# Decays as running products on VectorE, and the quarters of a product in other PSUM banks, in a scan layer followed by an ELU feed-forward layer

## The chip, the cores and the metric

The kernel runs on one core of one Trainium2 chip. The metric is device time in microseconds (us) of one execution. All matrices are fp32. The engines are named as in the profile: PE is TensorE (PEld its weight loads), DVE is VectorE, ACT is ScalarE, POOL is GpSimd, SP is the engine whose queue issues nearly all transfers.

## The reference, cut to what matters

```python
# x (4, 8, 768, 32), a (4, 8, 768) in 0.85..0.95, B and C (4, 8, 768, 16)
for c in range(24):                              # chunks of 32 tokens
    cum = np.cumsum(log(a)[chunk], axis=-1)
    L = np.exp(cum[..., :, None] - cum[..., None, :]) * causal
    y_intra = ((C @ B.T) * L) @ x
    y_inter = (C @ state) * np.exp(cum)[..., None]
    y[chunk] = y_intra + y_inter
    state = exp(sum(log a)) * state + sum_j(B_j x_j * exp(cum_last - cum_j))
h = y.transpose(0, 2, 1, 3).reshape(3072, 256) @ w_in      # w_in (256, 2048)
g = np.where(h > 0, h, np.exp(np.minimum(h, 0)) - 1)
out = g @ w_out                                            # w_out (2048, 256)
```

The entry L[i, j] of a chunk is the product of the decays a of the tokens j+1 to i, 1 where i is j, and 0 where i is before j. The chunk is free to choose as long as the state is carried right; the kernel uses chunks of 64.

## The kernel before, in words

**Blocks.** The 3072 tokens are cut into twelve blocks of 256, numbered n = 0 to 11. Each block is four chunks of 64 tokens (u and v, each 0 or 1) for eight heads. A block goes through two halves: the scan, which ends in `inside` (L542) with the turned output yT, and the feed-forward part, 8 steps i of 256 hidden columns each.

**The decays of a block.** For blocks 0 and 1 they are made from sums on PE and stay as they are. For blocks 2 to 11, `running_sums` (L273) takes cumulative sums F of log a once for all rows, `write_flat` (L308) puts them and their exponentials into DRAM, and `spread_cum` (L331) reads them back so that each of the 128 partitions (a token j) of the tile L holds the sums of all tokens i. `decay_of` (L436) then makes exp(cum_i - cum_j) by ACT, one instruction for each head and u with the sum of token j as the bias: 16 of 128x64 for a block (L439). POOL clears what lies before the diagonal with four `affine_select` of 64x512 for a block (L444). `ncum` and `eb`, the turned biases and the turned decays to the chunk's end, are made once (L906, L907). `scaled` (L359) multiplies B by the decay to the end, `weigh` (L463) multiplies the scores by L.

**The feed-forward part of blocks 0 to 3** is plain: `l1` (L577) makes a step's h, four matrix products of 128x256, and `l2` (L700) multiplies by w_out. In the trace each fp32 product is two matmul instructions.

**The feed-forward part of blocks 4 to 11** takes two blocks at a time (n = 4, 6, 8, 10) and does seven products in place of eight by Strassen's method in Winograd's form, for the first product in `front`, `front_sums`, `mid` and `back` (L660 to L692), for the second in `second` (L736). One step i of a pair of blocks is called a group here: there are 32 of them. A group has two PSUM banks, c1 and c2, of two quarters of 128x256 each. `front` issues three products and lets ACT copy the first of them. `front_sums` makes two sums by DVE in SBUF. `mid` issues two products and one DVE sum, `back` two products and two DVE sums. Only then are c1 and c2 both finished, and only then both enter the list `lag`, from which `elu` (L598) takes them: ACT makes relu(-h) (L596) and exp of it (L603), DVE makes g from this and h (L605).

**Order.** Everything is in the order in which the code is written (`manual_schedule`); each engine works through its own list in that order, and waits by semaphores. The loop at L1051 goes over the pairs, with 16 half steps k (k even: `front`, k odd: `mid` and `back`); between them it puts seven steps of `second` for the pair before (`l2s`), and what `scan_ahead` (L967) has for the next two blocks m and m+1: decays and the turning of B and C (`turn`, `turn_exp`) at k below 8, scores at k = 9, `weigh`, `sums` and `states` at k = 10 and 11, `across` and `inside` at k = 13. The pool of PSUM banks `p_a` has seven banks, taken in turn, so a new tile waits until the one seven takings before is free.

**Weights.** w_in and w_out come as fp64 words in 16 pieces, and are made fp32 by `w_take` (abs on ACT, the low word by L164 on ACT or L166 on DVE, the sign on DVE) and `w_give` (two DVE instructions L183 and L190, one sum L200 on POOL).

Of the kernel before, what the change touches and what calls it, by code (L numbers as in the profile page):

```python
# [10 lines left out]
F32 = mybir.dt.float32  # L11
# [17 lines left out]
def kernel(  # L29
# [234 lines left out]
    make_heads(1)  # L264

    def clip(t):
        nc.vector.tensor_scalar(
            out=t, in0=t, scalar1=1e-6, scalar2=1.0, op0=ALU.max, op1=ALU.min)
# [28 lines left out]
    F = const.tile([ROWS, 2, 2, P], F32, name="F")  # L297
    E = la

    def rest_of_sums():  # L300
        to_last(F[:, 0], E, nc.gpsimd)
        nc.scalar.activation(E, E, ACT.Exp)

# [26 lines left out]

    def spread_cum(n):  # L331

        st.setdefault(n, {})["L"] = L = att.tile([P, NH, 2, Q], F32, tag="L", name="L", bufs=2)
        for v in range(2):
            nc.sync.dma_start(
                out=L[Q * v:Q * v + Q].rearrange("p h u i -> p h (u i)"),
                in_=flat[v, rows_of(n)].rearrange("h u i -> h (u i)").unsqueeze(
                    0).to_broadcast([Q, NH, P]))

    def spread_exp(n):  # L340

        st.setdefault(n, {})["ec"] = ec = att.tile([P, 2, P], F32, tag="ec", name="ec", bufs=4)
        for h in range(NH):
            row = rows_of(n).start + NG * h
            nc.sync.dma_start(
                out=ec[N * h:N * (h + 1)].rearrange("n u i -> n (u i)"),
                in_=flat_exp[row:row + 1].to_broadcast([N, BLK]))

# [10 lines left out]
    def scaled(n, eng):  # L359

        s = st[n]
        s["sc"] = sc = att.tile([P, 2, NH, N], F32, tag="sc", name="sc", bufs=3)
        factor = eb0[:, :, NH * n:NH * (n + 1)] if n < 2 else eb[:, :, rows_of(n)]
        eng.tensor_tensor(
            out=sc, in0=s["bc"][:, 0],
            in1=factor.unsqueeze(3).to_broadcast([P, 2, NH, N]), op=ALU.mult)
# [64 lines left out]
    def decay(n, q):  # L431

        decay_of(n, 2 * q)
        decay_of(n, 2 * q + 1)

    def decay_of(n, h):  # L436
        L, row = st[n]["L"], rows_of(n).start + NG * h
        for u in range(2):
            nc.scalar.activation(  # L439
                L[:, h, u], L[:, h, u], ACT.Exp, bias=ncum[:, u, row:row + 1])  # L440
        if h % 4 == 3:
            for v in range(2):
                part = L[Q * v:Q * v + Q, h - 3:h + 1]
                nc.gpsimd.affine_select(  # L444
                    out=part, in_=part, pattern=[[0, 4], [0, 2], [1, Q]],
                    compare_op=ALU.is_ge, fill=0.0, base=0, channel_multiplier=-1)

# [212 lines left out]
    def front(n, i):  # L660
        c1, c2 = psum([P, 2, BLK], "ps_h"), psum([P, 2, BLK], "ps_h")
        t = y_sums[n]
        part_product(c1[:, 0], a11[:, i], yT[n // 2][:, 0, 0].rearrange("p u i -> p (u i)"), True)
        copy = conv.tile([P, BLK], F32, tag="sgn", name="p_copy")
        nc.scalar.copy(out=copy, in_=c1[:, 0])
        part_product(c2[:, 1], s_in[0][:, i], t[:, 1], True)
        part_product(c2[:, 0], a21[:, i], t[:, 0])
        open_[n, i] = c1, c2, copy

    def front_sums(n, i):  # L670
        c1, c2, copy = open_[n, i]
        u = conv.tile([P, 2, BLK], F32, tag="mag", name="u_sum")
        nc.vector.tensor_tensor(out=u[:, 0], in0=c2[:, 1], in1=copy, op=ALU.add)
        nc.vector.tensor_tensor(out=u[:, 1], in0=c2[:, 0], in1=u[:, 0], op=ALU.add)
        open_[n, i] = c1, c2, u

    def mid(n, i):
        c1, c2, u = open_[n, i]
        b21 = yT[n // 2][:, 1, 0].rearrange("p u i -> p (u i)")
        part_product(c1[:, 0], a12[:, i], b21)  # L680
        part_product(c1[:, 1], s_in[1][:, i], y_sums[n][:, 2])
        nc.vector.tensor_tensor(out=c2[:, 1], in0=c1[:, 1], in1=u[:, 1], op=ALU.add)  # L682

    def back(n, i):
        c1, c2, u = open_.pop((n, i))
        b22 = yT[n // 2][:, 1, 1].rearrange("p u i -> p (u i)")
        part_product(c1[:, 1], a22[:, i], y_sums[n][:, 3])
        part_product(c2[:, 0], s_in[2][:, i], b22)
        nc.vector.tensor_tensor(out=c1[:, 1], in0=c1[:, 1], in1=u[:, 0], op=ALU.add)  # L689
        nc.vector.tensor_tensor(out=c2[:, 0], in0=c2[:, 0], in1=u[:, 0], op=ALU.add)  # L690
        lag.append((n, i, c1))
        lag.append((n + 1, i, c2))  # L692
# [29 lines left out]
    def sub(out, in0, in1):  # L722
        nc.gpsimd.tensor_tensor(out=out, in0=in0, in1=in1, op=ALU.subtract)  # L723

    def sum_t1(n, i, eng=nc.gpsimd):
        b12 = g_of[n + 1, i][:, 0]
        eng.tensor_tensor(out=b12, in0=b12, in1=g_of[n, i][:, 0], op=ALU.subtract)  # L727

    def sum_t2(n, half):
        for i in range(4 * half, 4 * half + 4):  # L730
            t2_of[n, i] = ffn.tile([P, BLK], F32, tag="t2", name="t2", bufs=4)
            sub(t2_of[n, i], g_of[n + 1, i][:, 1], g_of[n + 1, i][:, 0])

    c_of = {}

    def second(n):  # L736
# [6 lines left out]
        for half in range(2):  # L743
# [8 lines left out]
            for r, a in enumerate((a11, a12, s1, s2, s3, a22, s4)):  # L752
                pool, tag = (p_a, "a") if (7 * half + r) % 2 else (p_o, "o")
                ps = pool.tile([P, 2, P], F32, tag=tag, name="ps_o")
                for i in chunk:
                    A, B = g_of[n, i], g_of[n + 1, i]
                    b = (A[:, 0], A[:, 1], B[:, 0], t2_of[n, i], A[:, 0], A[:, 1], B[:, 1])[r]
                    for ts in range(2):
# [6 lines left out]
                if r == 0:  # L765
                    nc.scalar.copy(out=p1, in_=ps)
                    for i in chunk:
                        sub(g_of[n, i][:, 0], t2_of[n, i], g_of[n, i][:, 0])
                    if half:
                        add(c11, c11, p1)  # L770
                elif r == 1:
                    add(c11, ps, c11 if half else p1)
                    for i in chunk:
                        sub(g_of[n, i][:, 1], g_of[n, i][:, 1], t2_of[n, i])
                elif r == 2:
# [61 lines left out]
    w_low(0, nc.scalar)  # L837
    log_of(la)
    scores(0)
# [21 lines left out]
    w_sum(1)  # L861
    running_sums(la, F[:, 0], ROWS)
    l1(0, 0)
# [4 lines left out]
    elu()  # L868
    nc.scalar.activation(F[:, 1], F[:, 0], ACT.Exp)
    write_flat()  # L870
    spread_cum(2)
    w_load(5)
# [15 lines left out]
    scaled(1, nc.gpsimd)  # L888
    rest_of_sums()
    w_give(3)  # L890
    make_heads(2)
    turn_exp(1)
    l1(0, 2)
# [11 lines left out]
    w_take(4, nc.vector)  # L905
    ncum = turned(F[:, 0], "ncum", -1.0, nc.vector)  # L906
    eb = turned(E, "eb", 1.0, nc.vector)  # L907
    w_give(4)
# [5 lines left out]
    for s, (n, i) in enumerate((  # L914
            (1, 0), (1, 1), (1, 2), (0, 4), (1, 3), (0, 5), (1, 4), (0, 6), (1, 5), (0, 7),
            (1, 6), (1, 7))):
        l1(n, i)
        if s < 8:
            decay_of(2, s)
        if s == 7:  # L920
# [3 lines left out]
        if s % 2 == 1 and todo < 10:  # L924
            w_take(todo, nc.vector)
            w_give(todo)
            w_load(todo + 6)
            todo += 1
        if s == 4:
            scaled(2, nc.gpsimd)  # L930
# [4 lines left out]
        if s == 8:  # L935
            spread_cum(3)
            load_x(3)
            spread_exp(3)
            weigh(2, 2)
            weigh(2, 3)  # L940

            st[0] = kept
            sums(2, 0, pool=p_o, tag="o", parts=(None, last))
            states(0, last)
            st.pop(0)
            states(2)
        if s == 10:
            spread_cum(4)
            inside(across(2), 2)
# [17 lines left out]
    def scan_ahead(n, i):  # L967
# [3 lines left out]
        if 4 < m < NP and n % 2 == 1 and i in (4, 5):  # L971
            spread_cum(m + i - 4)
        m = n + 2 - n % 2
        if 4 <= m < NP and n % 2 == 0:
# [3 lines left out]
            if i == 2:  # L978
                if m == 4:
                    spread_cum(5)  # L980
                load_x(m)
                load_x(m + 1)
            for k in (i,) if m == 4 else (i, i + 1) if i % 2 == 0 else ():
                if k >= 2:
                    decay(m + k // 6, (k - 2) % 4)
            if i in (5, 7):
                turn(m + i // 7)
                turn_exp(m + i // 7)
        if 4 <= m < NP and n % 2 == 1:
            if i == 0:  # L990
                scaled(m, nc.gpsimd)
                scaled(m + 1, nc.gpsimd)
            for k in (i,) if m == 4 else (i, i + 1) if i % 2 == 0 else ():
                if k < 2:
                    decay(m + 1, k + 2)
            if i == 2 and m == 4:
# [14 lines left out]
    for n in (2, 3):  # L1011
        for i in range(8):
            l2(n - 2, i)
            if todo < len(pieces):
                w_take(todo, nc.vector)
            end_of_two(n, 2 * i)
# [34 lines left out]
    for n in range(4, NP, 2):  # L1051
# [14 lines left out]
        for k in range(16):  # L1066
# [18 lines left out]
            elif m and i == 5:  # L1085
                l2s(2)
                mid(n, i)
                states(m)
                l2s(2)
                back(n, i)  # L1090
                states(m + 1)
                next_elu()
                begin_elu()
            else:
                mid(n, i)
                if i == 0 and n > 4:
                    store(n - 4, 0)
                    store(n - 4, 1)
                l2s(2)
                back(n, i)  # L1100

                if n == 4 and i < 4:
# [5 lines left out]
                l2s(1)  # L1108
                next_elu()
                begin_elu()  # L1110
            if m:
# [52 lines left out]
```

## Time and profile before

| | |
|---|---|
| median of 3 runs | 364.41 us (364.33 to 365.36) |
| span in the profile | 362.9 us |
| PE busy | 354.3 us, 98% |
| DVE, ACT, POOL busy | 242.2, 200.7, 227.1 us (67%, 55%, 63%) |
| decays by ACT, L439 | 160 instructions, 41.0 us |
| clearing by POOL, L444 | 40 instructions, 27.3 us |
| the low words by DVE, L166 | 12 instructions, 7.1 us |
| five sums of a group by DVE, L673, L674, L682, L689, L690 | 32 each, 13.5, 13.6, 13.8, 13.7 and 13.8 us |

Busy time of an engine is the union of its instructions. Matmuls overlap one another in the trace, so that PE is shown busy also where the next product has not been started as early as it could be; the distance from one start to the next tells more than the busy share.

### The profile page before, as it was taken

The numbers are of one execution on the slowest core, as the hardware profiler recorded it, in microseconds if no ns is written. First come the engines' busy times: TensorE is split into PE (matmuls) and PEld (weight loads), VectorE is DVE, ScalarE is ACT, GpSimd is POOL, SyncE is SP. The second block draws the span as 40 slices with busy tenths as digits, with TensorE's granted clock in tenths as the row PEclk, the third lists the DMA queues.
The fourth block names the chain that finished last, engine by engine and source line by source line (L and its number), as shares of the span: only waits on it lengthen the run. The fifth ranks groups of instructions, "written<-read, shape, count | busy, mean of one in ns | idle before, by whom it ended". The sixth has DMA issues, their size and how long they took to land.

```text
span 362.9 us, 10146 instructions
## 1 busy us (share of the span) xinstructions
PE 354.3 (98%) x3978; PEld 316.9 (87%) x3978; DVE 242.2 (67%) x547; ACT 200.7 (55%) x499; POOL 227.1 (63%) x366
## 2 busy tenths in 40 slices
PE   8899999999999999999999999999999999999996
PEld 5578778888888998898999998999989999999995
DVE  4989887972697668784567684666685666666212
ACT  4858969767435567635485735386735352534100
POOL 4454443663567896679457578567587555456893
PEclk9999999999999999999999999999999999999999
DMA  8877995563050560053530045540000100000001
GB/s 155 203 203 147 240 308 141 66 116 63 3 116 19 65 85 12 4 115 48 96 65 2 3 95 68 93 72 0 3 2 4 58 2 0 3 0 32 29 2 58
DMA packets 96239, 25.33 MB, mean 70 GB/s; under 512 B 77312, under 2 KB 92096, under 8 KB 96192
## 3 DMA queue, kind: packets, MB, share of 16 engines
q1 hardware_dynamic: 94016, 24.49, 33.0%
q8 instruction: 31, 0.51, 0.6%
q10 hardware_dynamic: 2176, 0.20, 0.4%
q14 instruction: 16, 0.13, 0.1%
HBM read 21.33 MB, written 3.34 MB: 68 GB/s over the span
## 4 chain that ended last, share of the span: by engine, by line
PE 81%; DVE 7%; ACT 3%; DMA 3%; SPq 2%; issue 2%; POOL 1%; ACTq 0%; DVEq 0%
PE ps_o L759 32%; PE ps_h L655 25%; PE ps_h L583 10%; PE ps_o L707 8%; SPq L112 2%; PE ps_g L459 1%; DMA w<-in_moe_w_in_dram 1%; DVE g L605 1%; PE ps_y L553 1%; ACT e L596 1%; PE ps_st L489 1%; ACT e L603 1%; DMA flat<-F 1%; DVE mag L183 1%; PE ps_y L534 1%
## 5 line engine op out<-in xcount | busy, mean ns | idle before, releaser
L596 ACT ACTIVATE e<-ps_h 128x512 f32<-128x512 f32 x96 | 56.5, 588 | 93.1 <-DVE ps_h L689 71.2
L605 DVE SCALAR_TENSOR_TENSOR g<-e,ps_h 128x512 f32<-128x512 f32 x96 | 65.3, 681 | 39.2 <-ACT e L603 35.8
L759 PEld LDWEIGHTS ps_o<-w_out,g 128*128 128x128 f32 x640 | 80.3, 192 | 3.3 <-issue 0.5
L759 PE MATMUL ps_o<-w_out,g 128*128 128x128 f32 x640 | 81.4, 275 | 0.0
L727 POOL TENSOR_TENSOR g<-g 128x256 f32<-128x256 f32 x34 | 24.8, 729 | 67.1 <-DVE g L605 67.1
L583 PE MATMUL ps_h<-yT,w_in 128*128 128x256 f32 x256 | 60.6, 383 | 2.5 <-POOL w_in L200 1.8
L603 ACT ACTIVATE e<-e 128x512 f32<-128x512 f32 x96 | 60.9, 634 | 2.2
L583 PEld LDWEIGHTS ps_h<-yT,w_in 128*128 128x128 f32 x256 | 47.8, 190 | 10.6 <-POOL w_in L200 2.8
L759 PE MATMUL ps_o<-w_sum,g 128*128 128x128 f32 x320 | 43.0, 275 | 0.0
L759 PEld LDWEIGHTS ps_o<-w_sum,g 128*128 128x128 f32 x320 | 41.1, 192 | 1.4
L439 ACT ACTIVATE L<-L,ncum 128x64 f32<-128x64 f32 x160 | 41.0, 338 | 0.0
L655 PE MATMUL ps_h<-y_sum,w_in 128*128 128x256 f32 x128 | 38.6, 383 | 0.7 <-DVE ps_h L682 0.7
L655 PE MATMUL ps_h<-y_sum,w_sum 128*128 128x256 f32 x128 | 38.5, 382 | 0.5 <-DVE g L605 0.5
L655 PE MATMUL ps_h<-yT,w_in 128*128 128x256 f32 x128 | 38.8, 385 | 0.0
L444 POOL TENSOR_SCALAR_AFFINE_SELECT L<-L 64x512 f32<-64x512 f32 x40 | 27.3, 682 | 13.1 <-ACT L L439 11.8
L707 PE MATMUL ps_o<-w_out,g 128*128 128x256 f32 x128 | 30.8, 383 | 0.0
L655 PEld LDWEIGHTS ps_h<-y_sum,w_sum 128*128 128x128 f32 x128 | 23.9, 190 | 5.3 <-DVE g L605 1.3
L723 POOL TENSOR_TENSOR g<-t,g 128x256 f32<-128x256 f32 x40 | 27.9, 729 | 0.8 <-PE ps_o L759 0.8
L723 POOL TENSOR_TENSOR t<-g 128x256 f32<-128x256 f32 x40 | 28.1, 736 | 0.2
L723 POOL TENSOR_TENSOR g<-g,t 128x256 f32<-128x256 f32 x40 | 27.9, 730 | 0.2
L707 PEld LDWEIGHTS ps_o<-w_out,g 128*128 128x128 f32 x128 | 23.7, 190 | 3.4 <-POOL L L444 0.2
L689 DVE TENSOR_TENSOR ps_h<-ps_h,u_sum 128x256 f32<-128x256 f32 x32 | 13.7, 429 | 18.3 <-PE ps_h L655 18.3
(109 smaller groups left out, 538.3 us busy)
## 6 DMA issues: line engine op xcount, KB each, us to landing
L<-flat SPq DMA_DIRECT2D x20, 256.0 KB, 5.3
w<-in_moe_w_in_dram SPq DMA_DIRECT2D x8, 512.0 KB, 5.2
w<-in_moe_w_out_dram SPq DMA_DIRECT2D x8, 512.0 KB, 6.1
xr<-in_x_dram SPq DMA_DIRECT2D x24, 128.0 KB, 3.4
out_dram<-c_sum SPq DMA_DIRECT2D x10, 256.0 KB, 2.1
bc<-in_B_dram SPq DMA_DIRECT2D x24, 64.0 KB, 4.4
bc<-in_C_dram SPq DMA_DIRECT2D x22, 64.0 KB, 3.4
ec<-flat_exp SPq DMA_DIRECT2D x72, 16.0 KB, 1.7
```

Source lines behind the costliest of these rows:

```text
L439: nc.scalar.activation(L[:, h, u], L[:, h, u], ACT.Exp, bias=ncum[:, u, row:row + 1])
L444: nc.gpsimd.affine_select(out=part, in_=part, pattern=[[0, 4], [0, 2], [1, Q]], compare_op=ALU.is_ge, fill=0.0, base=0, channel_multiplier=-1)
L583: nc.tensor.matmul(out=ps[:, j], lhsT=w_in[:, k, m * P:(m + 1) * P], rhs=yT[n // 2][:, k, n % 2].rearrange("p u i -> p (u i)"), start=(k = ...
L596: nc.scalar.activation(begun[0], lag[0][2], ACT.Relu, scale=-1.0)
L603: nc.scalar.activation(e, e, ACT.Exp, scale=-1.0)
L605: nc.vector.scalar_tensor_tensor(out=g_of[n, i], in0=e, scalar=1.0, in1=ps, op0=ALU.subtract, op1=ALU.max)
L655: nc.tensor.matmul(out=out, lhsT=lhsT, rhs=rhs, start=first, stop=True, skip_group_check=True)
L689: nc.vector.tensor_tensor(out=c1[:, 1], in0=c1[:, 1], in1=u[:, 0], op=ALU.add)
L707: nc.tensor.matmul(out=o_of[n][:, ts], lhsT=g_of[n, j][:, m % 2, ts * P:(ts + 1) * P], rhs=w_out[:, m], start=(m == 0 and ts == 0), stop=( ...
L723: nc.gpsimd.tensor_tensor(out=out, in0=in0, in1=in1, op=ALU.subtract)
L727: eng.tensor_tensor(out=b12, in0=b12, in1=g_of[n, i][:, 0], op=ALU.subtract)
L759: nc.tensor.matmul(out=ps[:, ts], lhsT=b[:, ts * P:(ts + 1) * P], rhs=a[:, i], start=(i == chunk[0] and ts == 0), stop=(i == chunk[-1]), s ...
```

## The change: what it does and what it is for

1. **Decays as running products.** `running_products` takes F[:, 1], the products of the a within a chunk, by one scan of a itself (no logarithm, no exponential), and F[:, 0], which is a with the first token of each chunk set to 0. The latter is spread over the partitions (`spread_a`). `decay` is then one DVE scan over two heads in place (state = state times a, plus `same`, which is 1 on the diagonal): it gives 0 before the diagonal, 1 on it and the products after it. Four of 128x256 for a block take the place of sixteen ACT and four POOL instructions. `ncum`, `eb` and four transposes are gone; `scaled` reads the last column of L. For two blocks at a time the scans are one in each half step k = 0 to 7.
2. **Low words on ACT.** The low words of pieces 5 to 15 (L164) move from DVE to ACT.
3. **Quarters in other banks, and joined sums.** c1 now is finished by the sum of `mid`, c2 by that of `back`. `front_sums` and the sum of `back` are one DVE instruction of 128x512 each instead of two of 128x256, so a group has three sums instead of five. c1 enters `lag` after `mid`, and its `elu` stands ahead of `back`.
4. **One transfer instead of eight** in `spread_exp`, and `sc` has two buffers instead of three.

```diff
-    def rest_of_sums():
-        to_last(F[:, 0], E, nc.gpsimd)
-        nc.scalar.activation(E, E, ACT.Exp)
+    nc.gpsimd.tensor_scalar(
+        out=F[:, 0], in0=keep[0:ROWS], scalar1=-1.0, scalar2=1.0, op0=ALU.mult, op1=ALU.add)
+    def running_products():
+        nc.vector.tensor_tensor_scan(
+            out=F[:, 1].rearrange("p c s -> p (c s)"),
+            data0=F[:, 0].rearrange("p c s -> p (c s)"),
+            data1=la.rearrange("p c s -> p (c s)"), initial=0.0, op0=ALU.max, op1=ALU.mult)
+        nc.gpsimd.tensor_tensor(out=F[:, 0], in0=la, in1=keep[0:ROWS], op=ALU.mult)
...
-        for h in range(NH):
-            row = rows_of(n).start + NG * h
-            nc.sync.dma_start(
-                out=ec[N * h:N * (h + 1)].rearrange("n u i -> n (u i)"),
-                in_=flat_exp[row:row + 1].to_broadcast([N, BLK]))
+        nc.sync.dma_start(
+            out=ec.rearrange("p u i -> p (u i)"),
+            in_=flat_exp[rows_of(n)].unsqueeze(1).to_broadcast([NH, N, BLK]))
...
-        factor = eb0[:, :, NH * n:NH * (n + 1)] if n < 2 else eb[:, :, rows_of(n)]
+        factor = (eb0[:, :, NH * n:NH * (n + 1)] if n < 2 else
+                  s["L"][:, :, :, Q - 1].rearrange("p h u -> p u h"))
...
-        decay_of(n, 2 * q)
-        decay_of(n, 2 * q + 1)
-    def decay_of(n, h):
...
+        part = st[n]["L"][:, 2 * q:2 * q + 2].rearrange("p k u i -> p (k u i)")
+        nc.vector.tensor_tensor_scan(
+            out=part, data0=part, data1=same.rearrange("p k i -> p (k i)"),
+            initial=0.0, op0=ALU.mult, op1=ALU.add)
...
-        copy = conv.tile([P, BLK], F32, tag="sgn", name="p_copy")
-        nc.scalar.copy(out=copy, in_=c1[:, 0])
-        part_product(c2[:, 1], s_in[0][:, i], t[:, 1], True)
-        part_product(c2[:, 0], a21[:, i], t[:, 0])
+        u = conv.tile([P, 3, BLK], F32, tag="mag", name="u_sum")
+        nc.scalar.copy(out=u[:, 0], in_=c1[:, 0])
+        part_product(c2[:, 0], s_in[0][:, i], t[:, 1], True)
+        part_product(c2[:, 1], a21[:, i], t[:, 0])
...
-        nc.vector.tensor_tensor(out=u[:, 0], in0=c2[:, 1], in1=copy, op=ALU.add)
-        nc.vector.tensor_tensor(out=u[:, 1], in0=c2[:, 0], in1=u[:, 0], op=ALU.add)
+        nc.vector.tensor_tensor(
+            out=u[:, 1:3], in0=c2, in1=u[:, 0].unsqueeze(1).to_broadcast([P, 2, BLK]), op=ALU.add)
...
     def mid(n, i):
-        part_product(c1[:, 1], s_in[1][:, i], y_sums[n][:, 2])
-        nc.vector.tensor_tensor(out=c2[:, 1], in0=c1[:, 1], in1=u[:, 1], op=ALU.add)
+        part_product(c2[:, 0], s_in[1][:, i], y_sums[n][:, 2])
+        nc.vector.tensor_tensor(out=c1[:, 1], in0=c2[:, 0], in1=u[:, 2], op=ALU.add)
+        lag.append((n, i, c1))
...
     def back(n, i):
-        part_product(c1[:, 1], a22[:, i], y_sums[n][:, 3])
-        part_product(c2[:, 0], s_in[2][:, i], b22)
-        nc.vector.tensor_tensor(out=c1[:, 1], in0=c1[:, 1], in1=u[:, 0], op=ALU.add)
-        nc.vector.tensor_tensor(out=c2[:, 0], in0=c2[:, 0], in1=u[:, 0], op=ALU.add)
-        lag.append((n, i, c1))
+        part_product(c2[:, 0], a22[:, i], y_sums[n][:, 3])
+        part_product(c2[:, 1], s_in[2][:, i], b22)
+        nc.vector.tensor_tensor(out=c2, in0=c2, in1=u[:, 0:2], op=ALU.add)
         lag.append((n + 1, i, c2))
...
-            w_take(todo, nc.vector)
+            w_take(todo, nc.scalar)
...
-            for k in (i,) if m == 4 else (i, i + 1) if i % 2 == 0 else ():
-                if k >= 2:
-                    decay(m + k // 6, (k - 2) % 4)
+            if m > 4:
+                decay(m + i // 4, i % 4)
+            elif i >= 2:
+                decay(m + i // 6, (i - 2) % 4)
...
                 mid(n, i)
+                begin_elu()
                 l2s(2)
+                next_elu()
                 back(n, i)
+                begin_elu()
...
                 l2s(1)
-                next_elu()
-                begin_elu()
```

## The prediction

> **What bounds the kernel now.** I read the chain first, then the starts of PE in a quiet stretch, then the waits of PE, then the busy time by stage. The page and its chain:
>
> ```profile
> PE 354.3 (98%) x3978; PEld 316.9 (87%) x3978; DVE 242.2 (67%) x547; ACT 200.7 (55%) x499; POOL 227.1 (63%) x366
> ...
> PE 81%; DVE 7%; ACT 3%; DMA 3%; SPq 2%; issue 2%; POOL 1%; ACTq 0%; DVEq 0%
> ```
>
> The end is set by PE. Whether it could be denser is read from the starts of one group (the timeline of PE):
>
> ```profile
> 123.55 0.60 PE L655 MATMUL ps_h<-yT,w_in 128*128 128x256 f32 x2
> 123.98 0.59 PE L655 MATMUL ps_h<-y_sum,w_sum 128*128 128x256 f32 x2
> 124.42 0.59 PE L655 MATMUL ps_h<-y_sum,w_in 128*128 128x256 f32 x2
> 124.85 1.95 PE L759 MATMUL ps_o<-w_out,g 128*128 128x128 f32 x16
> ...
> 129.70 0.60 PE L655 MATMUL ps_h<-yT,w_in 128*128 128x256 f32 x2
> ```
>
> A product of 256 columns starts every 0.434 us (two instructions of 0.216), a step of L759 every 0.445 (four of 0.111). A group is 7 x 0.434 + 7 x 0.445 = 6.15 us, and the trace has 129.70 - 123.55 = 6.15. So here PE has no slack, and no relief of another engine can bring anything. The change leaves PE's list as it is except for four small transposes. What it can bring lies only in starts that come late. Those with a wait behind them:
>
> ```profile
> PE ps_h L583 <- POOL w_in L200: 1.8, 2, 1.4
> PE ps_idle L215 <- DVE idle L210: 1.1, 1, 1.1
> PE ps_h L655 <- DVE ps_h L682: 0.7, 1, 0.7
> PE ps_h L655 <- DVE g L605: 0.5, 2, 0.3
> PE ps_h L583 <- DVE g L605: 0.4, 1, 0.4
> ```
>
> These idle times are short by the modelled end of the matmul before, so I took each start minus the usual distance from the start before. Beyond the first 12 us this gives nine late starts: 0.6 at 22.7 us, 0.65 at 43.2, 0.3 at 52.0, 0.25 and 0.83 at 139 to 142, 0.2 near 154, 0.36 at 167.6, 0.43 at 223.2, 0.21 at 265.1. Their sum is 3.8 us, 1% of the time, and that is the prize. The tail after the last matmul (3.5 us) is a sum and a store, and stays.
>
> How full the others are where the scans go (busy time in stretches; columns PE, PEld, DVE, ACT, POOL):
>
> ```profile
> 28.00:117.40 89.40, 88.84 (x1002) 75.48 (x1001) 69.53 (x147) 62.48 (x157) 47.66 (x75) 1.00 0.55 120
> 117.40:142.20 24.80, 24.13 (x166) 22.43 (x164) 17.10 (x38) 15.72 (x45) 21.93 (x35) 1.00 0.47 65
> ...
> 173.00:198.00 25.00, 25.00 (x173) 23.57 (x172) 16.44 (x36) 16.73 (x47) 14.68 (x22) 1.00 0.35 59
> ```
>
> **What the Trainium skill says.** "Perfetto Trace Analysis", Identifying the Most-Contended Engine: matmul busy share is no measure of the distance to the limit. The trace agrees: 98% busy and still 3.8 us late. "DVE: opcode table, instruction layouts, handler registers and perf-mode slots", Datapath and trigger behaviour: a scan runs at half throughput. The one scan of 128x256 here took 691 ns against 421 for a sum of that size. "SBUF — State Buffer", Who interferes with whom: a DVE instruction with two SBUF inputs and a POOL instruction that reads SBUF exclude each other for their whole length. The trace agrees: a sum L631 of 128x128 took 0.28 us with POOL quiet at 137.38 and 0.71 at 137.69 while POOL worked. The new scans have two SBUF inputs.
>
> **The change part by part.** Following instructions on DVE start about 0.08 us before the one ahead ends, so I use 0.60 for a row of 0.68, 0.33 for 0.42 and 0.61 for a scan of 0.69.
>
> ACT: minus 160 x 0.24 (the distance of L439 to L439) = 38 us, plus 11 low words at 0.77 (L164) = 8.5. POOL: minus 27.3, plus two sums at about 0.7. DVE: 40 scans x 0.69 = 27.6, minus 11 low words of 0.58 = 6.4, minus 32 x (0.42 + 0.42 - 0.68) x 2 = 10.2: plus 11 us. The new forms are not in the trace; a joined sum is bounded by 0.68 (L605, also 512 wide from PSUM) and 0.85 (two apart), I take 0.68.
>
> Start, to 28 us. The logarithm and exponential (0.42 each) leave ACT at places where it waits for PE; nothing. L282 (0.61 on POOL at 20.23) overlaps L183 on DVE, which takes 0.81 instead of about 0.45; without it the piece that PE waits for at 22.7 comes 0.3 sooner. Minus 0.3. The four transposes fill a stretch at 27.0 in which the next product waits for the copy of yT on ACT, which ends at 27.50; nothing.
>
> 28 to 117 us. A scan (0.61) takes the place of a low word (0.38 apart) on DVE; ACT gives up four L439 (0.96) and gets 0.68 for each. The wait at 43.2 is for a g after the fourth scan: plus 0.1. Around 52 only the low words go: minus 0.3. For blocks 3 to 5, eight scans of 4.9 us meet six low words of about 3 us less, but ACT's abs no longer stands behind eight L439, and POOL loses the L444; pieces come no later. Nothing. Fewer transfers in the queue of SP (8 x 0.46 us become one) bring L for block 5 sooner; nothing on PE.
>
> Groups from 117 us. The PE wait for `mid`'s sum is old: the product at 134.54 follows the sum that ended at 134.28, so DVE has 0.2 us of slack there. New is that the second product of `mid` waits for `front_sums`. Most of all, g of c1 now stands on DVE behind `mid`'s sum and waits 1.33 us for ACT (0.59 + 0.63 and gaps), with `back`'s sum, scans, `front_sums` and g of c2 queued behind it, and behind these the next `mid` sum. The cycle of waits of a group with scans: mid sum 0.47, relu and exp 1.30, g 0.60, back sum 0.72, relu of c2 0.49 and copy 0.42 on ACT (the scan of the odd half step, 0.61, lies beside them), front_sums 0.60, g 0.60, one sum of `second` 0.33, scan 0.61: 6.14, as much as PE needs. For pairs 6 and 8 (four groups each): nothing to 0.2 us lost each pair; I take 0.1. For pair 4 come the weight sums L631 (about 0.7 a group) and, in the last two groups, `ctm` and `cts` (0.93). Working through the DVE list of its first four groups with these numbers I get late starts of 0.1, 0.2, 0.4 and 0.6: 1.3 against the 1.1 that stands there now. Groups without scans need 5.5 us.
>
> The waits at 167.6, 223.2 and 265.1 are for a bank that g of the earlier c1 holds:
>
> ```profile
> 167.42 0.69 DVE L605 SCALAR_TENSOR_TENSOR g<-e,ps_h 128x512 f32<-128x512 f32 x1 [1.00 <-ACT e L603]
> 167.77 1.13 ACT L570 COPY yT<-ps_y 128x256 f32<-128x256 f32 x3
> 168.16 0.30 PEld L655 LDWEIGHTS ps_h<-y_sum,w_sum 128*128 128x128 f32 x2 [0.60 <-DVE g L605]
> ```
>
> With c1 finished by `mid`, this g is over some 2 us sooner. Minus 1.0.
>
> Sum: -0.3 + 0.1 - 0.3 + 0.2 (pair 4) + 0.2 (pairs 6 and 8) - 1.0 = -1.1, and a little from 154: 363.2 us.
>
> **The rivals.** (a) *The new DVE cycle sets the pace of the groups with scans.* For it: the cycle equals PE's 6.15 with no slack, and POOL can hold a scan up by as much as its 0.73 us. At 0.15 to 0.4 us for each of 12 groups this is 2 to 4.5 more than I count, 365 to 367.5; I put it at 366. Against it: POOL gives up 16 x 0.68 = 10.9 us in each of these stretches, so it is in the way in under half of the cases. (b) *Nothing happens.* New late starts of 1 to 2 us pay back the old: 364.4. For it: PE's list is the same, and it had only 3.8 us to gain. (c) *All late starts go.* ACT has 38 us less, POOL 27 less, and instructions on DVE that now meet POOL get shorter. If pair 4 and 43.2 come out clean as well: 364.4 - 2.8 = 361.6. Against it: DVE is given more in the very stretch in which it already made PE wait.
>
> **How the numbers follow.** My forecast, 363.2 (between 362.4 and 363.7), gets 0.34, (c) 0.20, (b) 0.25, (a) 0.21. The line for faster is 363.3: of my forecast some 0.28 lies below it and 0.06 above, so faster is 0.28 + 0.20 = 0.48, same 0.06 + 0.25 = 0.31, slower 0.21. The range reaches from under (c) to the middle of (a), 361.2 to 366.0. It leaves out an ACT and POOL relief that also shortens the first 12 us, and the upper half of (a).
>
> **What would show it.** Right: PE groups without scans stay 6.15 apart; no wait for g after `inside`; L605 waits on ACT for about 1.3 us once a group; late starts at 120 to 148 of about 1.3 us; scans near 0.69, some up to 1.3. Wrong: groups in 173 to 198 or 228 to 254 more than 6.3 apart (then (a) holds), or a longer wait of L583 or L707 before 117 us (then the DVE order of the weights is what I misjudged), or scans well over 0.7 with POOL quiet.

## The result, and the profile after

| | before | after |
|---|---|---|
| median | 364.37 us (364.06 to 365.36, 4 runs) | 369.63 us (368.89 to 370.14, 4 runs) |
| ratio | | 1.0136, 95% interval 1.0113 to 1.0159 |
| span in the profile | 362.9 us | 368.3 us |

The changed kernel is 1.4% slower, 6.4 us over the forecast and 3.6 us beyond the upper end of its range. First the busy line and the chain of the page after:

```profile
PE 355.8 (97%) x3974; PEld 316.9 (86%) x3974; DVE 249.9 (68%) x510; ACT 171.7 (47%) x347; POOL 206.7 (56%) x328
...
PE 69%; DVE 16%; ACT 5%; POOL 4%; issue 4%; DMA 1%; ACTq 0%; POOLq 0%; DVEq 0%
```

ACT gave up 29 us, as counted, and POOL 20, some 6 less than counted; none of it reached the end. DVE is busy only 8 us more than before, but its share of the chain has gone from 7% to 16% and PE's from 81% to 69%: DVE now sets the end in places where PE did. The same stretches as before (columns PE, PEld, DVE, ACT, POOL):

```profile
28.00:117.40 89.40, 87.62 (x994) 74.07 (x993) 71.51 (x149) 53.76 (x103) 35.03 (x57) 1.00 0.53 120
117.40:142.20 24.80, 24.34 (x161) 22.17 (x159) 17.93 (x34) 10.46 (x22) 22.07 (x32) 1.00 0.43 65
173.00:198.00 25.00, 24.77 (x167) 22.81 (x166) 18.62 (x33) 11.23 (x24) 14.97 (x20) 1.00 0.33 59
```

In 173 to 198 us PE was busy for 25.00 of 25.00 us before and now has gaps; DVE went from 16.44 to 18.62. Even so DVE is idle for a quarter of this stretch, so the sum of its work doesn't explain the gaps. The waits of PE for DVE, from the view of waits (total us, times, longest), stand where before there was one of 0.7:

```profile
PEld ps_h L655 <- DVE ps_h L680: 4.1, 9, 0.9
PE ps_h L655 <- DVE ps_h L680: 2.4, 6, 0.7
...
PEld ps_h L655 <- DVE u_sum L672: 1.9, 5, 0.8
...
PE ps_g L459 <- DVE ctm L391: 1.1, 1, 1.1
```

L680 is `mid`'s sum, L672 the joined sum of `front_sums`. The timeline of PE over one group of pair 6:

```profile
192.31 0.60 PE L655 MATMUL ps_h<-yT,w_in 128*128 128x256 f32 x2
192.74 0.59 PE L655 MATMUL ps_h<-y_sum,w_sum 128*128 128x256 f32 x2
193.17 1.05 PE L765 MATMUL ps_o<-w_sum,g 128*128 128x128 f32 x8
194.45 0.70 PE L655 MATMUL ps_h<-y_sum,w_in 128*128 128x256 f32 x2 [0.23 <-DVE ps_h L680]
194.99 0.59 PE L655 MATMUL ps_h<-yT,w_sum 128*128 128x256 f32 x2
```

Two steps of L765 take 2 x 0.445, so `back`'s first product was due at 193.17 + 0.89 = 194.06 and started at 194.45: 0.39 late. Its wait is for L680. In the kernel before, the same product of this group came on time, 0.89 after the start of its two steps:

```profile
190.35 1.05 PE L759 MATMUL ps_o<-w_sum,g 128*128 128x128 f32 x8
191.24 0.60 PE L655 MATMUL ps_h<-y_sum,w_in 128*128 128x256 f32 x2
```

What stood ahead of L680 on DVE in the changed kernel, and what POOL did (two timelines):

```profile
192.04 0.68 DVE L605 SCALAR_TENSOR_TENSOR g<-e,ps_h 128x512 f32<-128x512 f32 x1
192.64 0.42 DVE L756 TENSOR_TENSOR p_sum<-ps_o,p_sum 128x256 f32<-128x256 f32 x1
192.97 1.10 DVE L444 TENSOR_TENSOR_SCAN L<-L,same 128x256 f32<-128x256 f32 x1
194.00 0.40 DVE L680 TENSOR_TENSOR ps_h<-ps_h,u_sum 128x256 f32<-128x256 f32 x1
```

```profile
192.80 0.73 POOL L732 TENSOR_TENSOR g<-g 128x256 f32<-128x256 f32 x1 [2.78 <-DVE g L605]
```

The scan took 1.10 us, not 0.69. POOL's L732 (`sum_t1`, two inputs in SBUF) was released by g of c2, the L605 at 192.04, and began 0.17 us ahead of the scan; it had 0.56 us left to run then, and the scan took 0.42 more than alone. This is no chance meeting. The program emits g, then `sum_t1` for POOL, then one sum of `second`, then the scan, so DVE starts its own obstacle each time. Of the eight scans in the even half steps of pairs 6 and 8, six took 1.09 to 1.10 us. The two others had no sum of `second` between g and the scan; there DVE came first and POOL was held instead:

```profile
179.89 0.68 DVE L444 TENSOR_TENSOR_SCAN L<-L,same 128x256 f32<-128x256 f32 x1
```

```profile
180.05 1.04 POOL L732 TENSOR_TENSOR g<-g 128x256 f32<-128x256 f32 x1 [4.22 <-DVE g L605]
```

**Where the 5 us lie.** I set the starts of L583 and L655 after against those before, product by product. The difference at the last group is +4.96 us:

| place (time before) | predicted | measured |
|---|---|---|
| piece of weights, 23.3 | -0.3 | -0.23 |
| product at 27.5 (four transposes gone) | 0 | -0.38 |
| 38.9 to 39.8 | 0 | +0.29 |
| 43.8 | +0.1 | +0.80 |
| 52.6 to 55.3 | -0.3 | -0.44 |
| 66.9 (product waits from 64 on) | 0 | +1.12 |
| bank waits 167, 223, 265 | -1.0 | -0.54, -0.58, -0.29 |
| pair 4, other | +0.2 | +1.85 |
| pair 6, other | +0.1 | +1.46 |
| pair 8, other | +0.1 | +1.77 |

The rows add up to +4.83; small steps, in the first 21 us, at 51 and at 99, make the rest. So every gain came, the bank waits with 1.41 in all; the losses on DVE were many times what was predicted. Two rows can't be put to the change: slot, t1_late and scan_first (below) have the same program up to 117 us, and show no step at 38.9 and -0.65, +0.20 and -0.35 at 43.8. The other rows before 117 us repeat in all four traces (66.9: +1.03 to +1.16).

The largest loss ahead of the groups, at 64 us, in the timelines of DVE, POOL and PE:

```profile
62.23 0.68 DVE L605 SCALAR_TENSOR_TENSOR g<-e,ps_h 128x512 f32<-128x512 f32 x1
62.83 2.03 DVE L444 TENSOR_TENSOR_SCAN L<-L,same 128x256 f32<-128x256 f32 x2
64.79 0.66 DVE L391 TENSOR_TENSOR ctm<-ps_tc,hmask 128x512 f32<-128x512 f32 x1
```

```profile
62.46 1.27 POOL L200 TENSOR_TENSOR w_out<-mag,w_out 128x512 uint32<-128x512 uint32 x1 [3.40 <-DVE mag L190]
```

```profile
65.59 0.70 PE L459 MATMUL ps_g<-ctm,bt 32*64 32x128 f32 x32 [1.05 <-DVE ctm L391]
```

The scores of block 3 on PE wait for `ctm`, which is queued on DVE behind two scans of the same block, and the first of them (1.45 us of the 2.03) is held by the sum of a weight piece on POOL.

### The profile page after: what moved, and what is told of

The parts are those of the page before. It is cut to its first block, busy times and chain, and to the rows that moved or that the text cites. A ratio compares the mean times of both kernels' runs of the same rounds, so it can differ in the third digit from the quotient of the medians.

```text
span 368.3 us, 9759 instructions
## 1 busy us (share of the span) xinstructions
PE 355.8 (97%) x3974; PEld 316.9 (86%) x3974; DVE 249.9 (68%) x510; ACT 171.7 (47%) x347; POOL 206.7 (56%) x328
## 4 chain that ended last, share of the span: by engine, by line
PE 69%; DVE 16%; ACT 5%; POOL 4%; issue 4%; DMA 1%; ACTq 0%; POOLq 0%; DVEq 0%
PE ps_o L765 24%; PE ps_h L655 18%; PE ps_h L583 13%; PE ps_o L704 7%; DVE g L605 4%; DVE L L444 3%; PE ps_y L553 2%; ACT e L596 2%; POOL g L720 2%; PE ps_y L534 1%; ACT e L603 1%; DVE ps_h L688 1%; PE ps_g L459 1%; DVE u_sum L672 1%; DVE ctm L391 1%
## 5 line engine op out<-in xcount | busy, mean ns | idle before, releaser
L605 DVE SCALAR_TENSOR_TENSOR g<-e,ps_h 128x512 f32<-128x512 f32 x96 | 65.4, 681 | 49.4 <-ACT e L603 46.3
L765 PEld LDWEIGHTS ps_o<-w_out,g 128*128 128x128 f32 x640 | 80.3, 192 | 3.3 <-issue 0.5
L765 PE MATMUL ps_o<-w_out,g 128*128 128x128 f32 x640 | 81.4, 275 | 0.0
L732 POOL TENSOR_TENSOR g<-g 128x256 f32<-128x256 f32 x34 | 25.7, 758 | 77.6 <-DVE g L605 77.6
L583 PE MATMUL ps_h<-yT,w_in 128*128 128x256 f32 x256 | 60.5, 383 | 3.0 <-POOL w_in L200 1.9
L583 PEld LDWEIGHTS ps_h<-yT,w_in 128*128 128x128 f32 x256 | 47.8, 190 | 11.4 <-POOL w_in L200 3.3
L765 PE MATMUL ps_o<-w_sum,g 128*128 128x128 f32 x320 | 43.0, 275 | 0.1
L765 PEld LDWEIGHTS ps_o<-w_sum,g 128*128 128x128 f32 x320 | 41.1, 192 | 1.6 <-PE ps_o L765 0.2
L655 PE MATMUL ps_h<-y_sum,w_in 128*128 128x256 f32 x128 | 39.1, 387 | 2.4 <-DVE ps_h L680 2.4
L655 PE MATMUL ps_h<-y_sum,w_sum 128*128 128x256 f32 x128 | 38.5, 382 | 0.5 <-DVE u_sum L672 0.4
L655 PE MATMUL ps_h<-yT,w_in 128*128 128x256 f32 x128 | 38.7, 384 | 0.0
L672 DVE TENSOR_TENSOR u_sum<-ps_h,u_sum 128x512 f32<-128x512 f32 x32 | 21.9, 686 | 19.3 <-ACT u_sum L665 16.7
L444 DVE TENSOR_TENSOR_SCAN L<-L,same 128x256 f32<-128x256 f32 x40 | 33.9, 852 | 0.0
L720 POOL TENSOR_TENSOR g<-g,t 128x256 f32<-128x256 f32 x40 | 29.0, 755 | 0.0
L655 PEld LDWEIGHTS ps_h<-y_sum,w_sum 128*128 128x128 f32 x128 | 23.8, 190 | 5.0 <-DVE u_sum L672 1.9
L655 PEld LDWEIGHTS ps_h<-y_sum,w_in 128*128 128x128 f32 x128 | 21.8, 190 | 5.7 <-DVE ps_h L680 4.1
```

Source lines behind the costliest of these rows:

```text
L444: nc.vector.tensor_tensor_scan(out=part, data0=part, data1=same.rearrange("p k i -> p (k i)"), initial=0.0, op0=ALU.mult, op1=ALU.add)
L583: nc.tensor.matmul(out=ps[:, j], lhsT=w_in[:, k, m * P:(m + 1) * P], rhs=yT[n // 2][:, k, n % 2].rearrange("p u i -> p (u i)"), start=(k = ...
L605: nc.vector.scalar_tensor_tensor(out=g_of[n, i], in0=e, scalar=1.0, in1=ps, op0=ALU.subtract, op1=ALU.max)
L655: nc.tensor.matmul(out=out, lhsT=lhsT, rhs=rhs, start=first, stop=True, skip_group_check=True)
L672: nc.vector.tensor_tensor(out=u[:, 1:3], in0=c2, in1=u[:, 0].unsqueeze(1).to_broadcast([P, 2, BLK]), op=ALU.add)
L732: eng.tensor_tensor(out=b12, in0=b12, in1=b11, op=ALU.subtract)
```

## The experiments

Theory A: the place of the scans is at fault, behind the instruction that releases POOL's `sum_t1`, so that the scan takes 1.1 us and stands ahead of `mid`'s sum. Theory B: DVE has too much to do between two sums of `mid`, wherever the scans stand. Theory C: the loss is the new order of the joined sums. All times are medians; ratios are against the kernel before, run beside them.

| kernel | us | ratio, 95% interval |
|---|---|---|
| slot | 365.64 | 1.0020 (1.0006 to 1.0033) |
| t1_late | 368.89 | 1.0117 (1.0075 to 1.0159) |
| joined_only | 366.03 | 1.0032 (1.0015 to 1.0048) |
| scans_only | 375.29 | 1.0293 (1.0271 to 1.0315) |
| scan_first | 367.22 | 1.0072 (1.0056 to 1.0088) |
| slot_early | 364.47 | 0.9997 (0.9983 to 1.0011) |
| slot_turn | 364.50 | 0.9995 (0.9981 to 1.0009) |
| slot_low | 363.67 | 0.9978 (0.9966 to 0.9990) |
| copy_first | 361.98 | 0.9930 (0.9903 to 0.9958) |
| copy_turn | 362.88 | 0.9949 (0.9927 to 0.9970) |

### slot: both scans of a group where DVE waits for ACT

```diff
-            if m > 4:
-                decay(m + i // 4, i % 4)
-            elif i >= 2:
+            if m == 4 and i >= 2:
                 decay(m + i // 6, (i - 2) % 4)
...
                 begin_elu()
+                if m and i < 4:
+                    for j in (2 * i, 2 * i + 1):
+                        decay(m + j // 4, j % 4)
                 l2s(2)
                 next_elu()
                 back(n, i)
```

> For pairs 6, 8 and 10 of blocks both scans of a group stand behind the sum of mid, where DVE waits some 1.3 us for ACT, instead of one in each half step. Theory A (place: a scan in the even half step is held by the POOL sum that g of c2 releases, and stands in front of mid's sum): the late starts of groups 0 to 4 of n = 6 and n = 8 (1.4 us each) fall under 0.2, those of n = 4 (1.85) by at least 1; the time falls by 3 to 4 to about 366. Theory B (amount: DVE has too much to do in these groups wherever the scans stand): under 1 us is won, 369. Theory C (the joined sums and their new wait cost, not the scans): nothing is won.

Measured: 365.64 us. The late starts of pairs 6 and 8 fell to about 0.1 and 0.2 in one group each, pair 4 to nearly what it was before. The scans themselves got longer, from the groups by line and form (busy us, mean ns), here slot:

```profile
L444 DVE TENSOR_TENSOR_SCAN L<-L,same 128x256 f32<-128x256 f32 x40 | 36.0, 926 | 0.0
```

and the changed kernel:

```profile
L444 DVE TENSOR_TENSOR_SCAN L<-L,same 128x256 f32<-128x256 f32 x40 | 33.9, 852 | 0.0
```

So the same number of scans with more time in them costs little where DVE would wait for exp anyway. B falls: it is the place, in pair 4 too.

### t1_late: POOL's sum emitted one half step later

```diff
                 if at[0] % 2:
-                    sum_t1(at[0] - 1, at[1])
+                    late.append((at[0] - 1, at[1]))
...
                 mid(n, i)
+                late_t1()
```

> Only the POOL sum of g (sum_t1) moves, from right behind g of c2 to behind the next mid; the scans stay. Theory A in its strong form[...]: scans of the even half step fall from about 1.09 to 0.68 us, the late starts of n = 6 and n = 8 from 1.4 to about 0.4 each, the time by 2 to 3 to about 367. Theory B: scans get shorter but the late starts stay within 0.4 us of what they are. Theory C: nothing.

Measured: 368.89 us, mostly a miss of the edit itself. Being emitted later delays an instruction only if something is ahead of it in its own queue. POOL's queue was empty, and L732 still began as soon as g was there; of the six scans of 1.09 to 1.10 in pairs 6 and 8, four stayed so. In one group of each pair, where POOL had a sum of `second` to do first, L732 came behind it and the scan took 0.68. DVE and POOL there, in pair 6:

```profile
191.98 0.68 DVE L444 TENSOR_TENSOR_SCAN L<-L,same 128x256 f32<-128x256 f32 x1
192.57 0.41 DVE L680 TENSOR_TENSOR ps_h<-ps_h,u_sum 128x256 f32<-128x256 f32 x1
```

```profile
192.21 0.97 POOL L756 TENSOR_TENSOR p_sum<-p_sum 128x256 f32<-128x256 f32 x1 [6.32 <-DVE p_sum L756]
193.14 0.73 POOL L732 TENSOR_TENSOR g<-g 128x256 f32<-128x256 f32 x1
```

The late start of 0.49 (the product and the one behind it) went with it in both pairs. That speaks for the lock, but it is one group of each pair.

### scan_first: the clean test of the lock

The scan of the even half step stands ahead of g of c2 and so of the release of L732. Between the two sums of `mid`, DVE has the same instructions.

```diff
-            if m > 4:
+            if m > 4 and i % 2:
                 decay(m + i // 4, i % 4)
...
                     front_sums(n, i)
+                    if m and k < 8:
+                        decay(m + k // 4, k % 4)
                     next_elu()
```

> As the changed kernel, but in the even half steps the scan stands ahead of g of c2 instead of behind it, so that it has started before that g releases the sum of POOL (L732). The same instructions between the same two sums of mid. Theory A (the scan is slow because it always meets L732, which has started 0.17 us before): the scan falls from 1.10 to 0.68 us, L732 is held in its place, and of the late starts at mid's product in pairs 6 and 8 (0.16, 0.39 and 0.58 in each) at most 0.2 is left in each group; pair 4 loses some 0.8 as well; 366 to 367.5 us. Theory B (the amount of work of DVE between two sums of mid is too much in any case): the scan's length matters little, the late starts stay, 369 to 370 us.

Measured: 367.22 us, within A's range. DVE in the group that corresponds to the one shown above:

```profile
190.77 0.68 DVE L444 TENSOR_TENSOR_SCAN L<-L,same 128x256 f32<-128x256 f32 x1
191.37 0.66 DVE L605 SCALAR_TENSOR_TENSOR g<-e,ps_h 128x512 f32<-128x512 f32 x1
191.95 0.41 DVE L756 TENSOR_TENSOR p_sum<-ps_o,p_sum 128x256 f32<-128x256 f32 x1
192.28 0.42 DVE L680 TENSOR_TENSOR ps_h<-ps_h,u_sum 128x256 f32<-128x256 f32 x1
```

The same three instructions ahead of `mid`'s sum take 1.51 us from start to start (190.77 to 192.28), against 1.96 in the changed kernel (192.04 to 194.00), and `back`'s first product is on time again, 0.89 after its two steps:

```profile
192.00 1.05 PE L765 MATMUL ps_o<-w_sum,g 128*128 128x128 f32 x8
192.89 0.60 PE L655 MATMUL ps_h<-y_sum,w_in 128*128 128x256 f32 x2
```

Of the late starts in pairs 6 and 8 some 0.2 or less is left in a group. Pair 4 was a miss: its late starts stayed (0.44, 0.43, 0.76, 0.42). There the scan ahead of g met other sums of POOL (0.98 and 0.83 us in two groups), and DVE has two weight sums more in each group. Which of these counts was not tested; the amount of work alone does not make the loss, as slot has the same work in pair 4 and no loss over the kernel before.

### joined_only and scans_only: one part of the change alone

joined_only is the kernel before with part 3 (and two buffers of `sc`); scans_only is the changed kernel with the five sums and the old order of `front`, `mid`, `back` and `lag`.

The core of the sums in scans_only, against the changed kernel:

```diff
-        nc.vector.tensor_tensor(
-            out=u[:, 1:3], in0=c2, in1=u[:, 0].unsqueeze(1).to_broadcast([P, 2, BLK]), op=ALU.add)
+        nc.vector.tensor_tensor(out=u[:, 0], in0=c2[:, 1], in1=copy, op=ALU.add)
+        nc.vector.tensor_tensor(out=u[:, 1], in0=c2[:, 0], in1=u[:, 0], op=ALU.add)
...
```

> The kernel before with part 3 alone (quarters in other banks, joined sums, elu of c1 ahead of back), decays by ACT as before; sc with two buffers to make room. Theory A and B: part 3 is not what costs; the bank waits at 167, 223 and 265 go (0.5 each at the first two) and no new late start in groups with decays comes; about 363, 1 to 1.5 under before. Theory C: 1 us or more over before, with late starts behind front_sums.

> The changed kernel with part 3 taken back: five sums, both elu of a group behind back. Theory A: the scans still stand in front of mid's sum, but no g waits for ACT between mid and back, so the cycle is shorter: late starts in n = 6 and 8 under 0.7 us each, but the bank waits are back; 367 to 369. Theory B: as slow as the changed kernel or slower, since five sums take DVE longer than three: 370. Theory C: the time of before and the early losses of 1.25, 365.6.

Measured: 366.03 and 375.29 us, 1.3 and some 10.6 over the kernel before. For joined_only C had the size, but not the place; for scans_only B had the direction, and no theory the size. In joined_only the bank waits went (-0.35, -0.45) and three late starts of 0.47 to 0.60 came, at the step of the scores. ACT there:

```profile
203.15 2.03 ACT L439 ACTIVATE L<-L,ncum 128x64 f32<-128x64 f32 x8
205.09 0.58 ACT L596 ACTIVATE e<-ps_h 128x512 f32<-128x512 f32 x1
205.70 0.63 ACT L603 ACTIVATE e<-e 128x512 f32<-128x512 f32 x1
```

`mid`'s sum was ready at 204.14, but relu of c1 stood behind eight decays on ACT. Then g of c1 came at 206.36, 2.22 us after DVE had run dry, with `back`'s sum behind it and g of c2 only at 208.99; PE's product at 209.73 waited for that last g. Once c1's elu stands ahead of `back`, ACT has to be free there: part 3 needs part 1.

In scans_only the same held scan stands ahead of `mid`'s sum (DVE):

```profile
187.98 1.10 DVE L444 TENSOR_TENSOR_SCAN L<-L,same 128x256 f32<-128x256 f32 x1
189.00 0.40 DVE L682 TENSOR_TENSOR ps_h<-ps_h,u_sum 128x256 f32<-128x256 f32 x1
```

In the kernel before this sum had 0.2 us of slack; a scan of 1.02 ahead of it makes some 0.8 late, and late starts of 0.73, 0.74 and 1.33 stand in each of pairs 6 and 8. So C falls as the main cause: parts 1, 2 and 4 cost 10.6 without part 3, and with it 5.3 - 1.3, some 4 us more than part 3 alone.

### slot_early: `ctm` ahead of the scans as well

Beside slot, the turning of block 3 stands ahead of its scans, and the last scan of block 2 behind the elu.

```diff
                 if i < 2:
                     decay(3, 2 * i)
...
                 if i == 1:
+                    turn(3)
+                    turn_exp(3)
...
-                    turn(3)
-                    turn_exp(3)
```

> Both scans of a group between mid's sum and g of c1 (as in slot), and for blocks 2 and 3 the turned C (ctm, cts) and the elu ahead of the scans on DVE. If the late start of 1.1 us at 63 us is ctm of block 3 behind two scans on DVE, it goes, and 0.3 at 43 with it: 364.2 to 364.8 us, level with the kernel before. If it is the late transfer of a piece of weights or ACT that sets this start, it stays and the time is that of slot, 365.6.

Measured: 364.47 us. The step at 66.9 us, +1.03 in slot, is gone; the expectation that `ctm` behind two scans was its cause held. The 0.3 at 43 us did not go with it. The trace also loses 0.63 at 38.9 and 0.66 at 51.3, which the trace of slot does not, so the one step does not account for the medians by itself. This is the change with its scans and the turning of block 3 in other places, level with the kernel before.

### slot_low and slot_turn: part 2 undone, and `ctm` in the slot

slot_low against slot_early, in both places:

```diff
-            w_take(todo, nc.scalar)
+            w_take(todo, nc.vector)
```

slot_turn against slot_early:

```diff
-            if i in (5, 7):
+            if m == 4 and i in (5, 7):
...
+                if m and i == 4:
+                    for j in (m, m + 1):
+                        turn(j)
+                        turn_exp(j)
```

> As slot_early, but the low words of the weight pieces are made by DVE, as in the kernel before (part 2 of the change undone). If part 2 was needed to make room for the scans of blocks 3 to 5 on DVE, late starts of L583 between 40 and 60 us come back, 0.3 to 1 us more than slot_early. If it was of no use there, the time is the same within 0.3 us.

> As slot_early, and for pairs 6 to 10 the turning of B and C (transposes, bt, ctm, cts) of both blocks is put between mid's sum and g of c1 of step 4, where DVE waits for ACT and no scan stands. If the rest of the late starts in slot (0.96 at 139 us, 0.28 in each of pairs 6 and 8) are ctm and cts ahead of front_sums, and bt ahead of the copy that front_sums needs, they go: 1.2 to 1.5 us less than slot_early, 362.8 to 363.3 us, under the kernel before. If the four banks taken at once, or scores right behind, make PE wait: no gain or up to 1 us more, 364.4 to 365.5.

Measured: slot_low 363.67 us, 0.8 less than slot_early; neither expectation had part 2 as a loss. In the traces the difference lies before 117 us: slot_early has late starts of 0.53 at 38.8 and 0.86 at 52.2 that slot_low has not. slot_turn, the same program as slot_early up to there, has the second (0.85) and not the first. Both products wait for a g on DVE; what makes it late was not settled. The intervals of the two ratios overlap a little, so that the 0.8 is not sure. slot_turn gained nothing (364.50): in pair 4 late starts of 0.18 and 0.77 became 0.35 and 0.19, and in pairs 6 and 8 the joined sum, with `ctm` and `cts` out of its way, stood idle for the copy instead (DVE):

```profile
193.00 0.68 DVE L688 TENSOR_TENSOR ps_h<-ps_h,u_sum 128x512 f32<-128x512 f32 x1
194.61 0.69 DVE L672 TENSOR_TENSOR u_sum<-ps_h,u_sum 128x512 f32<-128x512 f32 x1 [0.93 <-ACT u_sum L665]
```

### copy_first and copy_turn: the copy ahead of relu

On ACT the copy L665 that the joined sum needs stood behind relu of c2, which waits for `back`'s sum. copy_first is slot_low with the two in the other order; copy_turn adds the edit of slot_turn.

```diff
                     front(n, i)
+                    if lag and not begun:
+                        begin_elu()
                     front_sums(n, i)
...
                 back(n, i)
-                begin_elu()
```

> As slot_low, but on ACT the copy of front's first product (L665) stands ahead of relu of the c2 before (L596), which waits for back's sum. In slot and slot_turn the joined sum L672 was idle for 0.3 to 0.9 us for that copy. If this wait makes the 0.28 us of late starts in each of pairs 6 and 8, they go: 363.1 us (0.5 less than slot_low). The 0.76 at 139 us in pair 4 (ctm, cts and weight sums L631 ahead of L672 on DVE without idle time) stays. If relu of c2, now later, holds up g of c2 and with it the next sum of mid, there is no gain: 363.5 to 364 us.

> As copy_first, with ctm, cts and bt of the next pair between mid's sum and g of c1 of step 4, as in slot_turn. slot_turn took half of the 0.77 at 139 us and left or moved the rest, as L672 waited for the copy there; with both edits the late starts of pairs 4 to 8 should be under 0.1 each: 0.6 to 1.2 us less than slot_low, 362.5 to 363.1. If the late starts are set by DVE's own list and not by the copy: 363.3 or more, no better than copy_first.

Measured: copy_first 361.98 us, under the expected 363.1 and 0.7% under the kernel before; copy_turn 362.88, with an interval that overlaps. In copy_first the copy comes early, and L672 follows on DVE without idle time (ACT, then DVE):

```profile
192.65 0.37 ACT L665 COPY u_sum<-ps_h 128x256 f32<-128x256 f32 x1 [0.28 <-PE ps_h L655]
193.89 0.60 ACT L596 ACTIVATE e<-ps_h 128x512 f32<-128x512 f32 x1 [0.86 <-DVE ps_h L688]
```

```profile
194.36 0.41 DVE L399 TENSOR_TENSOR cts<-ps_tc,ec 128x256 f32<-128x256 f32 x1
194.69 0.68 DVE L672 TENSOR_TENSOR u_sum<-ps_h,u_sum 128x512 f32<-128x512 f32 x1
```

Between 174 and 270 us its starts gain 1.02 us on the kernel before, those of slot_low 0.31. From 117 us to the last group it is 1.62 and 0.66. So the traces show 1.0 us of the 1.7 between the two ratios; the rest was not found. The trace of copy_first is of a run of 363.17 us, over its median, and single profiles of the same program differ by up to 0.7 us at 25 us. The 0.97 at 139 us in pair 4 stays in copy_first, as expected; copy_turn halves it (0.51).

## Why the prediction was wrong

- **The bound and the prize** held: quiet groups of PE are 6.15 us apart in both traces, and only late starts could be won. Its own sign of being wrong came too: in pair 6, `back`'s first products at 187.81 and 194.45 are 6.64 apart, more than 6.3.
- **The step that failed** is the cycle of a group with scans: "scan 0.61: 6.14, as much as PE needs", and with it "nothing to 0.2 us lost each pair; I take 0.1". The term scan 0.61 measured 1.03 (192.97 to 194.00) in the half step that counts. The whole cycle, from `mid`'s sum at 187.36 to the next at 194.00, measured 6.64; the other terms make 5.61 of it, against 5.53 in the prediction. It was then 0.49 longer than PE's 6.15, with no slack to take it. Pairs 6 and 8 lost some 1.4 each at these sums; in the last group of each, the scan of the odd half step (0.96), `ctm` and `cts` lie on the cycle as well. scan_first, which alters little but that term, cleared these groups. For pair 4 the forecast of 0.2 failed as well (1.85); what share of it is the held scan stays open, as scan_first left it and slot took it away.
- **Why the term was mis-sized.** The lock was known: "SBUF — State Buffer", Who interferes with whom, calls what DVE and POOL share an exclusive lock and says that the order of issue decides who is held up, and this trace agrees (1.10 held against 0.68, and L732 1.04 against 0.73 when DVE came first). The prediction priced it by POOL's share: "in the way in under half of the cases". That treats the meetings as random. What counts is which instruction releases the POOL sum, and how long before the scan; the order in which the program emits them tells the first of these. The reading "with POOL quiet at 137.38" missed the same point: a POOL sum (L723) began at 137.44, and the DVE sum was not held because it had started first.
- **Rival (a)** was what came about, with 366 for 369.6. It put 2 to 4.5 us more on the 12 groups with scans than the forecast's 0.4; the three pairs lost 5.1 in all, 4.7 more. Its 0.15 to 0.4 for a group was somewhat low (0.26 to 0.69 in three groups of pairs 6 and 8). It did not count the stretch before 117 us.
- **"Nothing" for the scans of blocks 3 to 5** failed. They were compared with the low words that left DVE, by amounts. The scans stood ahead of `ctm`, for which PE waits: +1.12, gone in slot_early. On the "plus 0.1" at 43.2 nothing is shown either way: +0.80 in this trace, and -0.65 to +0.20 in three others of the same program.
- **Low words**: "Around 52 only the low words go: minus 0.3." The size was about right (-0.44), the reason not: slot_low, with the low words back on DVE, has the same -0.44 there. No run shows a use of part 2; without it slot_low took 0.8 us less than slot_early.
- **Bank waits, minus 1.0**: right, and somewhat more (-0.54, -0.58 and -0.29); all three are gone.
- **The four transposes, "nothing"**: right. In both traces the next product waits for the copy of yT. The 0.38 arises ahead of them: before, PE's L534 waited 0.22 and 0.18 us for POOL's `Sx` (L511), and after it does not, so that all up to that copy comes sooner. The prediction had no term for this.
- The changed kernel and nine of the others, all with the joined sums, have +0.32 or +0.33 us at 275.6, ahead of the last group of pair 8; scans_only has not. In each of the ten traces PE's L534 waits 0.22 us there for POOL's `Sx`. It is made from `S_new`, which DVE makes behind g of c1 (g at 274.83, `S_new` at 276.04); in the kernel before it came first (270.55, g at 271.53). No run tested this apart.

## What to carry to other kernels

Where two engines exclude each other, don't price the meeting by their busy shares: look for which instruction releases the other engine's work, and what the first engine does next. Put long work for an engine where it waits anyway, behind what others wait for, and not just ahead of the result that the bounding engine needs; the change cost 5 us with its 40 scans in one place and nothing with them in another. Two parts of a change can need each other, so that neither tried alone tells what they do together.

## What the runs showed of the hardware that was not expected

- A DVE instruction that POOL keeps out is shown as begun: the held scan is one record of 1.10 us with no idle time ahead of it. Its length, not a wait, tells that it was held; the view of waits has nothing of it.
- An order in the program holds POOL back only by what is in POOL's own queue (t1_late); an instruction emitted half a step later began at the same moment, 0.76 us after the start of the g that releases it (g at 184.40, L732 at 185.16; in the changed kernel 192.04 and 192.80).
- A relu that waits for DVE holds a ready copy behind it on ACT. Out of its way, the copy began 1.24 us ahead of relu (192.65 and 193.89). With this copy first the kernel went from 0.2% to 0.7% under the one before; the 29 us that ACT gave up in the changed kernel had not made that one faster.
